# A list scheduler whose cost table counts more latency between engines and whose rule prefers matmuls of one shape

## The chip, the cores and the metric

One core of a Trainium2 chip runs the whole program. The metric is the device time of one execution in microseconds, as the median of several runs. The engines are PE (matmul), DVE, ACT, POOL, and SP, which here only issues DMA transfers.

## The reference

Attention with a mask by blocks of 64, and behind it a bilinear feed-forward network (FFN):

```python
# q, k, v: [8 batches, 8 heads, 576, 64], float32
scores = scale * np.matmul(q, k.transpose(0, 1, 3, 2))
mask = (pos[:, None] // 64) >= (pos[None, :] // 64)
scores = np.where(mask, scores, -1000000000.0)
attn = np.exp(scores - np.max(scores, axis=-1, keepdims=True))
attn = attn / (np.sum(attn, axis=-1, keepdims=True) + 1e-09)
x = np.matmul(attn, v)            # -> [4608 tokens, 512]
return ((x @ w_a) * (x @ w_b)) @ w_out      # d_ff = 1536
```

All sizes are float32; the kernel writes the output transposed, [512, 4608].

## The kernel before, in words

Products of the FFN are made in three matmuls each (hi by hi, hi by lo, lo by hi; `mm3`, with its matmul in L252), on operands split into a high and a low part. Attention's work is cut into 32 head pairs, four to a batch, numbered 0 to 31; a tile name such as `x2_6` says batch 2, head 6, which is pair 11. The first 10 pairs make their scores in plain float32 (matmuls `x2` in the rows of the order: two heads in one row), the later ones in three products (`x6`).

For one pair the steps are these. SP loads k and q (L420) and v (L425). ACT casts k (L485) and q (L477), POOL and DVE (L481) make the low parts; the first 10 pairs need no such cast. PE makes the scores in four blocks on 64 rows of its array: C3 (tile x, 512 keys) and C1 (tile y), then C2 (tile x, 448 keys) and C0 (tile y), all in L505. DVE takes maxima (L524, L540 and L541), ACT makes the exps e and e_s (L551), which also frees the score tile for a later block; DVE sums and inverts (L580 to L585), POOL scales e (L594). Pairs 0 to 4 then transpose e on PE (tile `tp`, L620) and ACT copies the result; from pair 5 on, DVE transposes 32 by 32 blocks (L599) and 16 transfers on SP's queue (L650, `at<-bl`, called D here) bring the blocks to their place. V, the product with v (L659, tile `av`, 60 half matmuls on 64 columns), ends the pair. ACT copies it out (L677, L678), ACT and POOL split it into xh and xl, and SP stores it (L692).

When a batch's four pairs are through, its FFN is made for 4 of 12 chunks of d_ff, in between the attention of later pairs: groups of four matmuls (`mm4`, in L714 to L729) that make tiles `ps0` and `ps1` (the products with w_a and w_b) and `pso` (with w_out). They have the lowest priority, so they fill PE where no step of attention is ready. The other 8 chunks make up a second stage, whose matmuls stand in L1065 and whose sums stand in L982 on DVE.

The order of all this is not written out but made by `plan()` (L360 to L406). Each operation is an `Op` with an engine, a list of those it depends on, a key (its priority) and a mode: 0 for the FFN and the transposes, 1 for scores (64 rows), 2 for V (64 columns). The table TOOK (L44 to L69) gives its duration and the lag until its result can be used. An operation is ready at the latest end of those it depends on, plus 0.3 us (SLACK) if it runs on PE and they don't. The planner goes forward in its own time, takes for the engine that comes first the ready operation of lowest key, and adds SWITCH where PE's mode changes. Every engine then runs its queue strictly in the planned order, at whatever pace the chip gives. `plan()` is called once for attention with the first part of the FFN (L938) and once, with `LOOK`, for the second stage (L1431), where all modes are 0. Between the two stands a piece of FFN whose order is written by hand.

Of the kernel before, what the change touches and what calls it, by code (L numbers as in the profile page):

```python
# [32 lines left out]
SLACK = 0.3  # L33
FIRST = 4
PET = 5
# [3 lines left out]
CONV_KEY = 12.0  # L39
CONV_LO = True  # L40
KEEP_UNTIL, KEEP_EVERY = 66.0, 2.5
SWITCH = 0.1
LAGS = {"PE": 0.24, "DVE": 0.14, "Activation": 0.17, "Pool": 0.1, "SP": 2.0}
TOOK = {  # L44
# [12 lines left out]
    "posta": (0.29, 0.17, 0), "postb": (0.375, 0.14, 0), "posto": (0.29, 0.17, 0), "hh": (0.338, 0.16, 0),  # L57
# [21 lines left out]
def attention_then_bilinear_ffn(  # L79
# [14 lines left out]
    DO, T = outT.shape  # L94
# [252 lines left out]
    PE_, DVE_, ACT_, POOL_, SP_ = LAGS  # L347
# [9 lines left out]
            self.n, self.frees, self.end = len(ops), None, None  # L357
            ops.append(self)

    def plan(look=0.0):  # L360
        free = dict.fromkeys(LAGS, 0.0)
        ready = {e: [] for e in LAGS}
        users = [[] for _ in ops]
        left = [len(o.deps) for o in ops]
        for o in ops:
            for d, plus in o.deps:
                users[d.n].append((o, plus))
            if not o.deps:
                ready[o.eng].append(o)
        out = []  # L370
        mode = 0
        bus = 0.0
        held = []

        def since(o):
            if not o.frees:
                return o.at
            if len(held) < MM:
                return o.at
            r = held[-MM]  # L380
            return o.at if r is o else 1e9 if r.end is None else max(o.at, r.end)

        while any(ready.values()):
            t, e = min((max(free[e], min(map(since, q))), e) for e, q in ready.items() if q)
            o = min((o for o in ready[e] if since(o) <= t + look), key=lambda o: (o.key, o.n))
            t = max(t, since(o))
            if o.frees:
                held.append(o.frees)
            ready[e].remove(o)
            free[e] = t + o.took + (SWITCH if e == PE_ and o.mode != mode else 0)  # L390
            if e == PE_:
                mode = o.mode
            if o.also:
                free[ACT_] = max(free[ACT_], t) + o.also
            o.start, o.end = t, free[e] + o.lag
            if o.kind in KB:
                bus = max(bus, t + LATENCY - 0.3) + KB[o.kind] / RATE
                o.end = bus + 0.3
            out.append(o)
            for u, plus in users[o.n]:  # L400
                u.at = max(u.at, o.end + plus + (SLACK if u.eng == PE_ and e != PE_ else 0))
                left[u.n] -= 1
                if not left[u.n]:
                    ready[u.eng].append(u)
        assert len(out) == len(ops)
        return out  # L406
# [37 lines left out]
    def got(what, p):  # L444
        return done.get((what, p))

    def attention(p):
# [9 lines left out]

        def add(what, eng, fn, deps=(), off=0.0, kind=None, **kw):
            deps = [(got(*d[:2]), *d[2:]) if isinstance(d, tuple) else (d,) for d in deps]
            done[what, p] = o = Op(kind or what, eng, fn, [(*d, 0.0)[:2] for d in deps if d[0]], key=B0 + off, **kw)  # L460
            return o

# [472 lines left out]
    for k in range(EARLY):  # L935
        o = Op("cv1", DVE_, lambda: next(box["g"]), [o, done["rc", NP - 1]], key=base[-1] + 20 + k)
    with tc.manual_schedule(engines={getattr(mybir.EngineType, e) for e in LAGS}):
        for o in plan():  # L938
            o.fn()
    conv2 = box["g"]  # L940
    lo_eng[0] = nc.vector
# [532 lines left out]
```

## Time and profile before

| what | us |
|---|---|
| median of 3 runs | 1134.1 (1132.92 to 1137.85) |
| profiled execution, its own time | 1138.72 |
| its span | 1136.9 |
| PE busy | 1096.3 (96%) |
| DVE busy | 871.4 (77%) |
| ACT busy | 630.0 (55%) |
| POOL busy | 402.7 (35%) |

The profiled execution is one that lies 4.6 us above the median of the runs; its mean granted PE clock is 0.987 of full speed. In the rows of a timeline stand start, duration, engine, line, operation, output and inputs with their sizes, the count, and in brackets the idle time ahead of it with what ended it. Line numbers are those of the kernel before.

### The profile page before, as it was taken

What the parts mean: (1) busy time and instruction counts of PE and PEld (TensorE: products, weight loads), DVE (VectorE), ACT (ScalarE), POOL (GpSimd) and SP (SyncE); (2) the same over time, 40 slices, a digit from 0 to 9 for tenths busy, and PEclk for the clock granted to TensorE, in tenths of its full rate; (3) what the DMA queues carried; (4) which work ended last, traced back from release to release, by engine and by line L of the source; (5) the groups of instructions that cost most, each with busy time, mean ns of one, the idle gap of its engine ahead of it and who ended that gap; (6) DMA issues with size and microseconds to landing.
All of it is one profiled execution on the core that took longest, in us unless ns stands there. A gap on an engine that the chain in (4) does not pass through costs nothing.

```text
span 1136.9 us, 23053 instructions
## 1 busy us (share of the span) xinstructions
PE 1096.3 (96%) x8356; PEld 1029.6 (91%) x8356; DVE 871.4 (77%) x1807; ACT 630.0 (55%) x1624; POOL 402.7 (35%) x593
## 2 busy tenths in 40 slices
PE   6889989999999999999999999999999999999997
PEld 3568778998988898899999999999999999999997
DVE  5888778776877777762899997787974877877856
ACT  4886566656665666662464654545543545545532
POOL 4687557664666556562100210202202022022020
PEclk7999989999999999999999999999999999999999
DMA  4553788877777887777433745737569245055052
GB/s 163 163 163 88 186 224 224 225 203 207 204 209 205 232 218 180 216 193 190 146 115 130 181 120 145 197 108 172 144 223 347 44 82 112 15 97 105 7 98 69
DMA packets 79024, 180.56 MB, mean 159 GB/s; under 512 B 13376, under 2 KB 34880, under 8 KB 78912
## 3 DMA queue, kind: packets, MB, share of 16 engines
q1 hardware_dynamic: 66240, 161.79, 48.5%
q0 software_dynamic: 12672, 17.31, 10.1%
q8 instruction: 66, 1.08, 0.4%
q14 instruction: 46, 0.38, 0.1%
HBM read 80.74 MB, written 48.76 MB: 114 GB/s over the span
## 4 chain that ended last, share of the span: by engine, by line
PE 58%; DVE 7%; DMA 6%; ACT 2%; SPq 2%; POOL 2%; issue 1%; ACTq 0%; POOLq 0%; DVEq 0%
PE bank L1065 46%; PE ps L252 5%; PE pso L252 3%; PE av L659 2%; DVE bl L599 2%; DMA kr<-kT 2%; DMA qr<-qT 2%; SPq L650 2%; DVE nm L524 1%; DMA at<-bl 1%; PE x L505 1%; POOL e L594 1%; PE y L505 1%; ACT e L551 1%; DVE xl L1017 1%
## 5 line engine op out<-in xcount | busy, mean ns | idle before, releaser
L1065 PE MATMUL bank<-xh,wab 128*128 128x384 f32 x1344 | 345.4, 334 | 0.8 <-DVE t L982 0.7
L1065 PEld LDWEIGHTS bank<-xh,wab 128*128 128x128 f32 x1344 | 243.0, 188 | 1.4 <-DVE t L982 1.0
L1171 POOL DMA_DIRECT2D outT<-pt x88 | 77.5, 1122 | 463.2 <-ACT pt L1329 275.7
L1065 PE MATMUL bank<-xl,wab 128*128 128x384 f32 x672 | 224.5, 334 | 0.0
L252 PE MATMUL ps<-xh,wab 128*128 128x288 f32 x1024 | 213.1, 298 | 0.0
L252 PEld LDWEIGHTS ps<-xh,wab 128*128 128x128 f32 x1024 | 165.4, 188 | 6.9 <-issue 5.5
L594 POOL TENSOR_SCALAR e<-e,rc 128x512 f32<-128x512 f32 (+3 forms) x256 | 150.5, 605 | 48.3 <-DVE rc L585 47.1
L252 PE MATMUL ps<-xl,wab 128*128 128x288 f32 x512 | 152.7, 298 | 0.0
L599 DVE STREAM_TRANSPOSE bl<-e 128x512 f32<-128x512 f32 (+1 forms) x216 | 116.4, 584 | 14.0 <-POOL e L594 12.7
L1065 PEld LDWEIGHTS bank<-xl,wab 128*128 128x128 f32 x672 | 126.1, 188 | 0.0
L982 DVE TENSOR_TENSOR u<-bank,u 128x384 f32<-128x384 f32 x158 | 87.8, 556 | 46.7 <-PE bank L1065 40.2
L1065 PE MATMUL bank<-hz,wo 128*128 128x384 f32 x612 | 109.9, 334 | 0.0
L1065 PEld LDWEIGHTS bank<-hz,wo 128*128 128x128 f32 x612 | 106.4, 188 | 0.0
L659 PEld LDWEIGHTS av<-at,v 128*64 128x64 f32 x1920 | 95.1, 140 | 8.4 <-issue 3.9
L659 PE MATMUL av<-at,v 128*64 128x128 f32 (+1 forms) x1920 | 100.2, 262 | 1.8 <-DMA at<-bl 1.1
L252 PE MATMUL pso<-hh,wo 128*128 128x288 f32 x480 | 101.3, 300 | 0.0
L252 PEld LDWEIGHTS ps<-xl,wab 128*128 128x128 f32 x512 | 96.1, 188 | 4.0 <-issue 3.4
L505 PE MATMUL x<-k,q 64*128 64x512 f32 (+1 forms) x344 | 65.7, 477 | 22.9 <-ACT e L551 18.7
L982 DVE TENSOR_TENSOR t<-bank,t 128x384 f32<-128x384 f32 x98 | 54.4, 555 | 38.8 <-ACT t L1108 20.3
L252 PEld LDWEIGHTS pso<-hh,wo 128*128 128x128 f32 x480 | 78.5, 190 | 3.2 <-issue 2.6
L524 DVE TENSOR_REDUCE nm<-x 128x2 f32<-128x1024 f32 x64 | 73.2, 1144 | 9.0 <-PE x L505 8.1
L551 ACT ACTIVATE e<-y,nm 128x192 f32<-128x192 f32 (+1 forms) x128 | 61.9, 486 | 22.0 <-DVE nm L524 18.5
(135 smaller groups left out, 1952.0 us busy)
## 6 DMA issues: line engine op xcount, KB each, us to landing
at<-bl SPq DMA_DIRECT2D x432, 112.0 KB, 2.3
xr<-xd SPq DMA_DIRECT2D x48, 384.0 KB, 4.2
outT<-pt POOLq DMA_DIRECT2D x88, 192.0 KB, 6.4
cv<-wab SPq DMA_DIRECT2D x24, 512.0 KB, 5.1
v<-vm SPq DMA_DIRECT2D x32, 320.0 KB, 3.2
xd<-xf SPq DMA_DIRECT2D x32, 288.0 KB, 2.5
outT<-ob SPq DMA_DIRECT2D x64, 144.0 KB, 2.1
wabd<-st SPq DMA_DIRECT2D x8, 896.0 KB, 5.8
```

The source lines that it names most:

```text
L252: nc.tensor.matmul(ps, w_, d_, start=(i == 0), stop=(i == n - 1))
L505: nc.tensor.matmul(out[:, h], qq[r, q0[t]:q0[t] + P], keys, start=j == 0, stop=j == len(qk) - 1)
L524: nc.vector.tensor_reduce(st["nm"][:, :, t], view, axis=AX.X, op=ALU.max, negate=True)
L551: nc.scalar.activation(out, view, AF.Exp, bias=bias, accum_out=sm[:, h, t, :1])
L594: nc.gpsimd.tensor_scalar(ev, ev, st["rc"][:, h, t:t + 1], 1.0, op0=ALU.mult, op1=ALU.mult)
L599: nc.vector.transpose(dst, es[h][t].rearrange("p (c g q) -> p c g q", g=NQ, q=QB))
L650: nc.sync.dma_start(st["at"][QB * g:QB * (g + 1), i], bl[QB * i:QB * (i + 1), g])
L659: nc.tensor.matmul(out[d], v[:, h, c], a[:, qs, h, e_], start=start, stop=stop, skip_group_check=True)
L982: return lambda: v.tensor_tensor(o, a, b, op=op)
L1017: lambda h_=h_, l_=l_, src=src, eng_=eng_: eng_.tensor_tensor(l_, src, f32(h_), op=ALU.subtract),
L1065: nc.tensor.matmul(banks[bk], a, b, start=start and not i, stop=i == 3 * n - 1, skip_group_check=not start)
L1171: do("acc", POOL_, lambda: nc.gpsimd.dma_start(part[o * P:(o + 1) * P, ts], t, accum_op=ALU.add), [name], [("part", o, 2 * tt_ + j)], key= ...
```

## The change

Three things change in the planner, and no operation is added or removed. First, the constants: SWITCH goes from 0.1 to 0.15 us, `mm4` from 0.528 to 0.532, and a new table CROSS adds 0.2 us to every edge from PE, DVE, ACT or POOL to another engine; edges from SP, the loads and copies, get 0.0. Second, `plan(stay=True)` for attention: while PE's mode isn't 0, it prefers an operation of the same mode that is ready within 0.3 us (STAY), then one of the other nonzero mode, and only then what the old rule takes. In mode 0 the new line, with HOLD at 0, takes what the old rule takes, apart from operations that aren't ready yet. Third, OFF can replace an operation's priority; it is empty and does nothing.

```diff
-SWITCH = 0.1
+SWITCH = 0.15
+STAY, HOLD = 0.3, 0.0
+CROSS = {"PE": 0.2, "DVE": 0.2, "Activation": 0.2, "Pool": 0.2, "SP": 0.0}
+OFF = {}
...
-"mm4": (0.528, 0.24, 0),
+"mm4": (0.532, 0.24, 0),
...
-    def plan(look=0.0):
+    def plan(look=0.0, stay=False):
...
             t, e = min((max(free[e], min(map(since, q))), e) for e, q in ready.items() if q)
-            o = min((o for o in ready[e] if since(o) <= t + look), key=lambda o: (o.key, o.n))
+            near = [o for o in ready[e] if since(o) <= t + look]
+            if e == PE_ and stay:
+                if mode:
+                    near = [o for o in ready[e] if o.mode == mode and since(o) <= t + STAY] or [
+                        o for o in ready[e] if o.mode and since(o) <= t + STAY] or near
+                else:
+                    near = [o for o in near if not o.mode or since(o) <= t - HOLD] or near
+            o = min(near, key=lambda o: (o.key, o.n))
...
-                u.at = max(u.at, o.end + plus + (SLACK if u.eng == PE_ and e != PE_ else 0))
+                u.at = max(u.at, o.end + plus + (SLACK if u.eng == PE_ and e != PE_ else 0) + (CROSS[e] if u.eng != e else 0))
...
+            off = OFF.get("Tb" if what == "T" and p < PET else what, off) if what not in ("V0",) else off
...
-        for o in plan():
+        for o in plan(stay=True):
```

In the rows below, the number ahead of the operation is its line; lines of the changed file are 3 to 11 higher than those of before. Numbers at the end of tile names only count tiles. What moves is shown at three places.

PE's queue at the scores of pair 6 (batch 1, head 4), before:

```order
L505 MATMUL x1_4_0_1136<-k1_4_880,q1_4_889 128x512 x2
L252 MATMUL ps1_0_0_1_1128<-xl0_2_0_616,wab1_83 128x288
L252 MATMUL ps1_0_0_1_1128<-xh0_2_0_615,wab1_83 128x288
L252 MATMUL ps1_0_0_1_1128<-xh0_4_0_797,wab1_83 128x288
L252 MATMUL ps1_0_0_1_1128<-xl0_4_0_798,wab1_83 128x288
L505 MATMUL y1_4_4_1156<-k1_4_880,q1_4_889 128x128 x2
L505 MATMUL y1_4_4_1156<-k1_4_880,q1_4_889 128x320 x2
```

and now:

```order
L516 MATMUL x1_4_0_1124<-k1_4_900,q1_4_905 128x512 x2
L516 MATMUL y1_4_1_1135<-k1_4_900,q1_4_905 128x128 x2
L516 MATMUL y1_4_1_1135<-k1_4_900,q1_4_905 128x320 x2
L255 MATMUL ps0_0_0_1_1116<-xl0_2_0_626,wab1_83 128x288
L255 MATMUL ps0_0_0_1_1116<-xh0_2_0_625,wab1_83 128x288
L255 MATMUL ps0_0_0_1_1116<-xh0_4_0_813,wab1_83 128x288
```

Four FFN products no longer stand between C3 and C1. At C1 the FFN is 16 products less far (four of ps0_0_0_1 are done where all twelve and eight of ps1_0_0_1 were), and at V(4) it is still 16 behind. Something of the same kind happens at pair 9 (batch 2, head 2): before, C3, V(6), C1, 12 products, C2, C0; now C3, C1, V(6), 20 products, C2, 4 products, C0.

PE's queue ahead of V(9), the product of pair 9 (av2_2), before:

```order
L252 MATMUL ps0_1_0_3_2359<-xh1_4_0_1808,wab3_85 128x288
L252 MATMUL ps0_1_0_3_2359<-xh1_6_0_1937,wab3_85 128x288
L252 MATMUL ps0_1_0_3_2359<-xl1_6_0_1938,wab3_85 128x288
L252 MATMUL ps0_1_0_3_2359<-xh1_6_0_1937,wab3_85 128x288
L659 MATMUL av02_2_2387<-at2_2_2135,v2_2_2042 64x64 x2
L659 MATMUL av2_2_2386<-at2_2_2135,v2_2_2042 64x128 x8
```

and now, with the last scores of pair 11 (batch 2, head 6):

```order
L255 MATMUL ps0_1_0_2_2302<-xl1_0_0_1310,wab2_84 128x288
L255 MATMUL ps0_1_0_2_2302<-xh1_0_0_1309,wab2_84 128x288
L255 MATMUL ps0_1_0_2_2302<-xh1_2_0_1544,wab2_84 128x288
L516 MATMUL y2_6_5_2309<-k2_6_2024,q2_6_2035 128x192 x6
L670 MATMUL av02_2_2321<-at2_2_2074,v2_2_2043 64x64 x2
L670 MATMUL av2_2_2320<-at2_2_2074,v2_2_2043 64x128 x8
```

Before, 32 FFN products stand between the last scores of pair 11 and V(9); now none does. 88 products stand between V(8) and V(9) before, 60 now. On SP's queue the loads of pair 12 stood ahead of the 16 copies of pair 9, and now stand behind them. On DVE the split of q for pair 13 (L481) stood ahead of pair 12's maximum (L524) and now stands behind all of pair 12's maxima.

ACT's queue at the exps of pair 16 (batch 4, head 0) and the cast of k for pair 17 (batch 4, head 2), before:

```order
L551 ACTIVATE e0_1_0_104,sm0_137<-y4_0_1_3438,nm4_0_3451 128x320
L756 CAST hh_2_0_3_3549<-hf_2_0_3_3534 128x288
L551 ACTIVATE e0_s_117,sm0_137<-y4_0_1_3438,nb4_0_3453 128x128
L485 CAST k4_2_3487<-kr4_2_3488 128x576
L551 ACTIVATE e0_1_1_108,sm0_137<-y4_0_1_3438,nm4_0_3451 128x320
```

and now:

```order
L562 ACTIVATE e0_1_0_104,sm0_137<-y4_0_4_3408,nm4_0_3397 128x320
L562 ACTIVATE e0_1_1_108,sm0_137<-y4_0_4_3408,nm4_0_3397 128x320
L496 CAST k4_2_3484<-kr4_2_3485 128x576
L488 ACTIVATE q4_2_3489<-qr4_2_3490 128x640
L562 ACTIVATE e0_2_0_105,sm0_137<-x4_0_5_3527,nm4_0_3397 128x448
```

Both exps of tile y now stand ahead of the cast. Casts of k that stand ahead of an exp of the first two blocks (e_3, e_1 or e_s) of the pair before are those of pairs 12, 17, 19, 24 and 28 before, and of pairs 14, 18, 19, 20, 24 and 28 now.

2 rows, old and new, of the table TOOK are left out of this document.

## The prediction

> **What bounds the kernel now.** I read the execution first by its stages, in a table of windows: start, end and length, then the busy time of PE, its weight load, DVE, ACT and POOL, then PE's granted clock. The stages are the opening, the front (pairs 5 to 9, up to the first FFN product of the second batch), the rest of attention, and the second stage.
>
> ```profile
> 0.00:80.00 80.00, 62.63 (x490) 40.91 (x492) 61.51 (x125) 57.90 (x175) 50.17 (x85) 0.91 0.49 159
> 80.00:158.30 78.30, 72.21 (x626) 58.41 (x624) 60.57 (x137) 48.41 (x156) 48.21 (x75) 0.93 0.59 161
> 158.30:533.70 375.40, 365.05 (x3705) 335.03 (x3703) 269.37 (x626) 223.27 (x709) 222.96 (x343) 1.00 0.78 208
> 533.70:1131.00 597.30, 596.30 (x3543) 595.26 (x3540) 478.33 (x918) 300.40 (x585) 81.38 (x92) 1.00 0.49 127
> ```
>
> PE is the bound everywhere but in the opening. Its idle time, most of what a new order can give back, is 78.30 − 72.21 = 6.1 us in the front, 375.40 − 365.05 = 10.4 us in the rest of attention and 597.30 − 596.30 = 1.0 us in the second stage. The front shows another loss: a clock of 0.93. So the next view was PE alone in narrow windows (length, PE's busy time, clock):
>
> ```profile
> 113.90:117.30 3.40, 1.54 (x11) 1.00 0.79 178
> 117.30:120.70 3.40, 3.40 (x17) 0.50 0.69 156
> 144.60:148.00 3.40, 1.14 (x9) 1.00 0.84 235
> 148.00:154.90 6.90, 5.54 (x42) 0.51 0.85 241
> 260.70:264.10 3.40, 1.35 (x20) 1.00 0.92 248
> 264.10:267.50 3.40, 3.40 (x41) 0.50 0.50 112
> ```
>
> Three times PE has under half of a 3.4-us window to do and runs the next window (once two) at half clock. A late operation thus costs its wait and then up to half of 3.4 us.
>
> **The change, part by part.** It adds and removes no instruction; the counts by engine are equal, and only the order differs. The larger SWITCH and the rule of the same shape ought to save changes of shape on PE. They hardly exist as a saving: counted in PE's order there are 203 stretches of one shape before and 202 after. From the timeline of PE (start, length) a change pair's price is seen where four FFN products stand between the two score blocks of pair 6:
>
> ```profile
> 93.01 1.13 PE L505 MATMUL x<-k,q 64*128 64x512 f32 x4
> 94.07 0.40 PE L252 MATMUL ps<-xl,wab 128*128 128x288 f32 x1
> ...
> 94.79 1.03 PE L505 MATMUL y<-k,q 64*128 64x128 f32 x8
> 99.41 0.42 PE L252 MATMUL ps<-xh,wab 128*128 128x288 f32 x2
> ...
> 99.81 0.43 PE L252 MATMUL ps<-xh,wab 128*128 128x288 f32 x2
> ```
>
> Three products in a row (two, and the one in the line left out) take 99.81 − 99.41 = 0.40 us, 0.133 each, so four take 0.53; between the score blocks they take 94.79 − 94.07 = 0.72. Two changes cost 0.19 us, one stretch fewer about 0.1: I put it at 0 (0 to −0.2). What counts is where the waits go.
>
> *The front.* The rows of PE, then of SP's queue (start, time over which the group was issued):
>
> ```profile
> 103.42 2.99 PE L659 MATMUL av<-at,v 128*64 128x64 f32 x60
> 116.31 1.02 PE L505 MATMUL x<-k,q 64*128 64x448 f32 x4 [1.86 <-ACT e L551]
> 123.11 2.98 PE L659 MATMUL av<-at,v 128*64 128x64 f32 x60
> 149.37 1.87 PE L505 MATMUL x<-k,q 64*128 64x448 f32 x4 [3.63 <-ACT e L551]
> 151.80 4.44 PE L659 MATMUL av<-at,v 128*64 128x64 f32 x60
> 156.17 0.97 PE L505 MATMUL x<-k,q 64*128 64x512 f32 x6
> 158.31 0.40 PE L252 MATMUL ps<-xh,wab 128*128 128x288 f32 x1
> ```
>
> ```profile
> 106.50 2.16 SPq L650 DMA_DIRECT2D at<-bl  x3
> 117.82 1.14 SPq L650 DMA_DIRECT2D at<-bl  x2
> 126.13 1.15 SPq L650 DMA_DIRECT2D at<-bl  x2
> 149.81 0.58 SPq L420 DMA_DIRECT2D kr<-kT  x1
> ```
>
> The sixteen copies D of pair 5 start when V of pair 4 ends (103.42 + 2.99 = 106.4) and are issued until 118.96 (117.82 + 1.14); those of pair 6 start when V of pair 5 ends (126.1), those of pair 7 follow without a gap until 149.8, and then come the loads that C3 of pair 10 needs at 156.17. This chain, V(4), D(5), V(5), D(6), D(7), loads and V(7), C3(10), sets the end of the front. What the new order moves in it:
> V(4) has 16 FFN products fewer ahead of it (the old order has come to the fourth matmul of ps1_0_0_3, the new to the last of ps1_0_0_2), 16 × 0.133 = 2.1 us, if C2(6) is ready for it. Between C1(6) and C2(6) stand 40 products before and after, and before C2(6) didn't wait. I take −1.8; if the exps that free the score tiles set the pace there, only the four products moved out from between C3 and C1 are left, −0.7.
> V(5) comes 123.11 − 118.96 = 4.2 us after the last issue of its copies, which land in 2.3 us in the median (below); so 1.9 us of it are not the DMA's, but come from the wait of 1.86 and the half clock behind it. In the new order 44 products stand ahead of C2(7) where there were 36: 8 × 0.133 = 1.06 of the 1.86 are filled, and the window is no longer under half. I take another −1.8, so V(5) and with it SP's 23.7 us of copies (126.1 to 149.8) move by −3.6.
> V(7) ran in the window of half clock, 4.44 us where V(5) took 2.98. In the new order the wait of 3.63 us in C2(9) is covered by 20 products and V(6), which now stand between C1(9) and C2(9) where 12 products stood. But PE that is early there only waits for D(7): what it gains is the slower clock's 1.5 us, and of these the loads of pair 10, which land no sooner than their queue lets them, leave perhaps 0.4. Front: −4.0 (−1 to −7; the far end takes V(7)'s 1.5 and the opening's operations too). The FFN work done by 158.31 is the same set in both orders, so this shift is a gain and not borrowed.
>
> ```profile
> at<-bl SPq DMA_DIRECT2D x432, 112.0 KB, 2.3
> ```
>
> *The middle.* The place with the largest loss, ACT's timeline and PE's:
>
> ```profile
> 261.44 0.67 ACT L485 CAST k<-kr 128x576 fp32r<-128x576 f32 x1 [2.30 <-DMA kr<-kT]
> 262.02 0.52 ACT L551 ACTIVATE e<-y,nm 128x320 f32<-128x320 f32 x1
> ```
>
> ```profile
> 262.69 0.58 PE L505 MATMUL y<-k,q 64*128 64x192 f32 x6 [2.05 <-ACT e L551]
> 263.20 4.92 PE L659 MATMUL av<-at,v 128*64 128x64 f32 x60
> ```
>
> A cast of k waits 2.30 us for its load at the head of ACT's queue; the exp behind it frees the tile for C0(16), which waits 2.05; then V runs at half clock, 4.92 − 2.98 = 1.9 lost. The new order puts both exps ahead of the cast: −3.9.
>
> At pairs 9 to 12 the order of three queues changes. Before, DVE takes its split of q of pair 13 ahead of pair 12's maximum, and the block C2(12) waits for the exps; now the split comes after it. Also, 32 FFN products stood between pair 11's last scores and V(9); now none does, and the loads of pair 12 come behind the sixteen copies of pair 9 instead of ahead of them. PE's rows and SP's:
>
> ```profile
> 184.56 2.98 PE L659 MATMUL av<-at,v 128*64 128x64 f32 x60
> 196.55 0.89 PE L505 MATMUL x<-k,q 64*128 64x448 f32 x6 [1.31 <-ACT e L551]
> ```
>
> ```profile
> 168.17 0.33 SPq L420 DMA_DIRECT2D kr<-kT  x1
> 169.23 1.78 SPq L650 DMA_DIRECT2D at<-bl  x3
> 177.47 4.90 SPq L650 DMA_DIRECT2D at<-bl  x7
> ```
>
> The 1.31 in C2(12) goes. But V(9) now has 60 products between V(8) and itself and not 88, so PE reaches it 28 × 0.133 = 3.7 us sooner, in the times of before at 180.8, while pair 9's copies end 169.23 − 168.17 = 1.1 us sooner, at 181.3, and land some 1.7 after the start of the last (2.3 from its issue): V(9) waits until about 183.0, 2.2 us. Twelve products and V(9) lie ahead of C3(12), 183.0 + 2.98 + 1.6 = 187.6; its loads, issued at 181.3, are ready for PE 156.17 − 149.81 = 6.4 later, at 187.7, so they add nothing. Net +0.9 (−1.3 if the copies are quicker, +2.6 with a half clock of 1.7 behind the wait).
>
> Then the casts. The planner counts nothing more for SP's loads (0.0), so it goes on putting casts of k at a time at which the load hasn't landed. Casts ahead of an exp of the pair before that belongs to its first two blocks, as at pair 17, are those of pairs 12, 17, 19, 24 and 28 before, and of 14, 18, 19, 20, 24 and 28 now: three new ones, 14, 18 and 20. The rows of the waits in this stage (total, times, longest):
>
> ```profile
> ACT k L485 <- DMA kr<-kT: 14.0, 11, 2.4
> PE x L505 <- ACT e L551: 3.0, 4, 1.3
> PE y L505 <- ACT e L551: 2.7, 2, 2.0
> ```
>
> Of the 22 casts of pairs 10 to 31, 11 wait; 14.0 / 22 = 0.64 is what one waits on average, and I let it reach PE in full, +1.9 for three; the ends are 0 and 3 × 2.4 = +7.2. Middle: −3.9 + 0.9 + 1.9 = −1.1. The near end takes pair 12's −1.3, no wait of the casts and the other waits of PE for an exp, 3.0 + 2.7 − 2.05 − 1.31 = 2.3: −7.5. The far end has +2.6 and casts of 1.1 each: +2.0.
>
> *The second stage.* PE's order there, 3540 matmuls, is word for word the same; CROSS only moves DVE's, ACT's and POOL's operations. PE's idle ahead of its costliest group shows the slack:
>
> ```profile
> L1065 PE MATMUL bank<-xh,wab 128*128 128x384 f32 x1344 | 345.4, 334 | 0.8 <-DVE t L982 0.7
> ```
>
> There is next to nothing to gain; an operation moved behind another can cost its 0.5 us a few times: +0.5 (−0.5 to +2). The opening is a chain between engines that the order hardly shortens: 0 (±0.3).
>
> Sum: −4.0 − 1.1 + 0.5 = −4.6. On the profiled execution's 1138.7 this gives 1134.1 (only by chance the number of the median); that execution lies 4.6 above the median of the runs, so against the median of 1134.1 the forecast is 1129.5. Its ends: −7 − 7.5 − 0.5 = −15, 1119, and −1 + 2 + 2 = +3, 1137.
>
> **The rivals.** First, half clock stays. Windows lie on a grid in time; shift PE's work by 2 to 4 us and other windows fall under half. Then the 1.9 us behind C0(16) and the 1.8 us of V(5) do not come back: −4.6 + 3.7 = −0.9, 1133.2. For it: the 10.4 us of idle in the middle stay spread, and SP's loads set the pace. Against it: the three windows above belong to single long waits that the new order covers. The Trainium skill ("TensorE: Matmul & The Clock Gate", Part 1, "HAM oscillation — how this bites in real kernels") gives as its abstract rule no PE idle gaps over about 3.4 us. By that rule waits of 1.86 and 2.05 us would not be what halves the clock, and shortening them would return the waits alone, which is this rival's sum; the rows above, with half clock after 1.54 and 1.35 us of work in 3.4, speak against the rule. Chance 0.17.
>
> Second, slower. The casts of k for pairs 14, 18 and 20 wait 2.4 us each at the head of ACT's queue, with C0 behind, and PE's window falls under half as it did at 262.69, 1.9 more each: 3 × 4.3 = 12.9 in place of 1.9, and the sum is −4.6 + 11.0 = +6.4, 1140.5. It decides where the load lands some 2 us or more after the cast's turn, at all three places. That 11 casts wait now speaks for it; that their mean is 1.27, and that only one place in the trace cost as much as 3.9, speaks against it. Chance 0.10.
>
> Third, all goes. If both half clocks, every wait of the exps and the casts' waits vanish, and the front reaches −6: −6 − 7.5 + 0.5 = −13, 1121. For it: in the new order V(6) and 20 products, 5.6 us, stand between C1(9) and C2(9), and 40 or more products between most others from pair 6 on, where pair 9 had 12, 1.6 us. Against it: the loads and V(9). Chance 0.22.
>
> That the rule of the same shape does little, as the count 202 has it, is not a rival but part of the sum: the time would come from CROSS.
>
> **How the numbers follow.** The forecast has 0.51, the rivals 0.17, 0.10 and 0.22. About 0.5% (5.7 us, 1128.4 and 1139.8) is what a measurement of this kernel can tell from no change. The forecast lies 1.1 above the first bound, so of its 0.51 somewhat under half, 0.23, is faster; with the third rival faster has 0.45, same 0.28 + 0.17 = 0.45, slower 0.10. The range 1119 to 1137 holds the forecast's ends, the first rival and the third, and leaves out the second.
>
> **What the profile will show.** Right: the first product of the second batch starts near 154 us instead of 158.31; V of pair 5 near 119.5; no clock of 0.50 from 117 to 155 and none after C0(16); the second stage as long as before within 2 us. Wrong: V(5) where it was, so that the front's chain starts earlier than I think; other windows at 0.50; no wait ahead of V(9); PE waiting over 2 us for an exp behind a cast of k at pairs 14, 18 or 20; idle of over 3 us on PE in the second stage.

## The result and the profile after

The changed kernel is slower. Its median over 10 runs is 1142.8 us (1137.9 to 1151.3) where the kernel before has 1136.4 (1132.9 to 1139.5) on the same chips; the ratio is 1.0067, with a 95% interval of 1.0046 to 1.0088 (that of the medians alone is 1.0056, inside it). The forecast was 4.6 us faster. The profiled execution took 1147.0 us (span 1145.2), 8.3 us of span more than the one of before. One execution of a kernel further down (`att_pe`) ran at a granted clock of 0.65 and took 1513.8 us, where its eleven others took 1134 to 1144; ratios and the table of starts leave it out.

Where the 8.3 us come from is read from the same table of windows as in the prediction, cut this time at events and not at times: the start of C3 of pair 6, the start of C3 of pair 10, the end of the last V, the end. Before (start and end, length, PE busy, weight load, DVE, ACT, POOL, PE's clock):

```profile
0.00:93.00 93.00, 75.23 (x576) 50.60 (x576) 73.13 (x147) 69.96 (x211) 60.58 (x99) 0.93 0.48 156
93.00:156.20 63.20, 57.72 (x523) 47.48 (x522) 47.97 (x111) 34.70 (x116) 37.19 (x59) 0.92 0.62 164
156.20:533.70 377.50, 366.95 (x3723) 336.27 (x3721) 270.35 (x630) 224.92 (x714) 223.57 (x343) 1.00 0.78 208
533.70:1136.90 603.20, 596.46 (x3543) 595.26 (x3540) 479.91 (x921) 300.40 (x585) 81.38 (x92) 1.00 0.49 128
```

And now, at the same events:

```profile
0.00:104.70 104.70, 81.96 (x566) 54.11 (x566) 73.75 (x149) 71.25 (x212) 63.17 (x99) 0.85 0.43 139
104.70:165.90 61.20, 56.85 (x533) 48.50 (x532) 46.34 (x113) 34.03 (x117) 37.83 (x61) 0.94 0.66 172
165.90:539.20 373.30, 364.65 (x3724) 334.64 (x3720) 268.79 (x626) 224.78 (x712) 221.23 (x342) 1.00 0.79 210
539.20:1145.20 606.00, 598.43 (x3544) 594.99 (x3540) 473.66 (x921) 300.28 (x585) 81.51 (x92) 1.00 0.48 127
```

The opening is 11.7 us longer, the front 2.0 shorter, the middle 4.2 shorter and the second stage with the hand-ordered piece before it 2.8 longer: 11.7 − 2.0 − 4.2 + 2.8 = 8.3. DVE, ACT and POOL are busy for as long as before in the opening, within 3 us; they have no more to do. On PE the 11.7 us are two things. Its idle time grows from 17.8 us (93.00 − 75.23) to 22.7 (104.70 − 81.96), by 5.0 us. Its busy time grows by 6.7 us, although 12 FFN products fewer (1.6 us) are done in it, and the granted clock falls from 0.93 to 0.85: PE does less work and does it more slowly.

The place where the largest part of it arises is the turn from pair 2 to pair 3. PE's timeline there (`...` stands for rows left out), before:

```profile
36.68 1.13 PE L505 MATMUL x<-k,q 64*128 64x512 f32 x4
37.64 0.93 PE L505 MATMUL y<-k,q 64*128 64x128 f32 x8
...
43.54 1.02 PE L505 MATMUL x<-k,q 64*128 64x448 f32 x4 [0.97 <-ACT e L551]
...
46.33 0.57 PE L620 MATMUL tp<-ident,e_s 128*128 128x128 f32 x2 [0.43 <-ACT at L626]
46.79 1.05 PE L914 MATMUL keep<-z 128*128 128x512 f32 x2
47.95 2.99 PE L659 MATMUL av<-at,v 128*64 128x64 f32 x60
50.86 1.13 PE L505 MATMUL x<-k,q 64*128 64x512 f32 x4
```

And after:

```profile
34.51 1.13 PE L516 MATMUL x<-k,q 64*128 64x512 f32 x4
35.57 2.99 PE L670 MATMUL av<-at,v 128*64 128x64 f32 x60
38.48 1.03 PE L516 MATMUL y<-k,q 64*128 64x128 f32 x8
...
44.93 1.02 PE L516 MATMUL x<-k,q 64*128 64x448 f32 x4 [1.53 <-ACT e L562]
...
49.36 0.45 PE L631 MATMUL tp<-ident,e_s 128*128 128x128 f32 x1 [0.46 <-ACT at L637]
49.54 2.93 PE L925 MATMUL keep<-z 128*128 128x512 f32 x4
52.40 4.94 PE L670 MATMUL av<-at,v 128*64 128x64 f32 x60
57.27 1.13 PE L516 MATMUL x<-k,q 64*128 64x512 f32 x4
```

C3 of pair 2 starts 2.2 us sooner than before and C3 of pair 3 6.4 us later: 22.8 us for the pair instead of 14.2. C3(2) has overtaken V(0), C1(2) comes behind V(0), C2(2) waits longer for an exp, the last transpose of pair 1 comes 3 us later, four keep matmuls instead of two stand ahead of V(1), and V(1) runs at half clock (4.94 us for 2.99). The waits come first here: C2(2) is already 1.4 us late when the clock halves at 46.3 us (windows below). On DVE one sees why the exps are late. Its timeline ahead of pair 2's exps, before:

```profile
37.86 1.23 DVE L524 TENSOR_REDUCE nm<-x 128x2 f32<-128x1024 f32 x1 [0.19 <-PE x L505]
...
39.82 1.16 DVE L524 TENSOR_REDUCE nm<-y 128x2 f32<-128x256 f32 x2
...
41.50 0.16 DVE L541 TENSOR_REDUCE nb<-nm 64x4 f32<-64x8 f32 x1
```

And after:

```profile
35.78 1.17 DVE L535 TENSOR_REDUCE nm<-x 128x2 f32<-128x1024 f32 x1
36.86 0.68 DVE L910 SCALAR_TENSOR_TENSOR cv<-cv 128x512 int32<-128x512 int32 x1
37.64 0.91 DVE L912 TENSOR_TENSOR cv<-cv 128x512 f32<-128x512 f32 x1
38.59 0.76 DVE L903 TENSOR_SCALAR cv<-cv 128x512 int32<-128x512 int32 x1
39.26 0.43 DVE L906 TENSOR_SCALAR cv<-cv 128x512 int32<-128x512 int32 x1
39.72 0.93 DVE L908 SCALAR_TENSOR_TENSOR cv<-cv 128x512 f32<-128x512 uint16 x1
...
41.39 1.16 DVE L535 TENSOR_REDUCE nm<-y 128x2 f32<-128x256 f32 x2
...
42.83 0.16 DVE L552 TENSOR_REDUCE nb<-nm 64x4 f32<-64x8 f32 x1
```

Between the maximum of tile x and that of tile y, where only three small clearings of y stood, DVE now makes five operations of a weight conversion (`cv`). Weights are converted in the opening, on DVE, ACT and POOL, with a lower priority than attention; the FFN's first product needs them. The maximum of y ends its row at 42.5 us where it ended at 41.0, though its x came 2 us sooner.

Windows of PE in the kernel after (start and end, length, PE busy, PE's clock):

```profile
42.80:46.20 3.40, 1.57 (x7) 1.00 0.50 161
46.30:56.50 10.20, 9.29 (x58) 0.50 0.39 129
77.00:80.40 3.40, 1.21 (x7) 1.00 0.02 7
80.40:83.80 3.40, 3.35 (x12) 0.50 0.00 0
155.50:158.90 3.40, 1.40 (x12) 1.00 0.86 238
158.90:165.70 6.80, 4.99 (x54) 0.50 0.94 252
```

Half clock now falls into the opening, where before it had none between 25 us and 117 us. In all, PE runs at half clock for 17.9 us between 25 us and C3(6) (the windows at 46 and 80 us and one at 97 us).

### The profile page after: what moved, and what is told of

Read it like the earlier page. It is cut to its first block, busy times and chain, and to the rows that moved or that the text cites. A ratio compares the mean times of both kernels' runs of the same rounds, so it can differ in the third digit from the quotient of the medians.

```text
span 1145.2 us, 23065 instructions
## 1 busy us (share of the span) xinstructions
PE 1101.9 (96%) x8356; PEld 1032.2 (90%) x8356; DVE 862.5 (75%) x1807; ACT 630.3 (55%) x1624; POOL 403.7 (35%) x593
## 4 chain that ended last, share of the span: by engine, by line
PE 48%; DVE 3%; DMA 0%; issue 0%; ACT 0%; POOL 0%; SPq 0%; DVEq 0%; POOLq 0%
PE bank L1076 45%; PE ps L255 2%; PE pso L255 1%; DVE xl L1028 1%; DMA pt<-outT 0%; DVE u L993 0%; DVE cv L216 0%; DVE hz L1129 0%; DVE t L993 0%; DVE cv L194 0%; DVE wab L223 0%; DVE cv L1152 0%; DVE cv L192 0%; DVE cv L1154 0%; DVE wo L1159 0%
## 5 line engine op out<-in xcount | busy, mean ns | idle before, releaser
L670 PEld LDWEIGHTS av<-at,v 128*64 128x64 f32 x1920 | 96.9, 142 | 14.2 <-issue 8.5
L670 PE MATMUL av<-at,v 128*64 128x128 f32 (+1 forms) x1920 | 102.5, 264 | 7.1 <-DMA at<-bl 6.0
L535 DVE TENSOR_REDUCE nm<-x 128x2 f32<-128x1024 f32 x64 | 73.5, 1148 | 12.0 <-PE x L516 10.8
L562 ACT ACTIVATE e<-y,nm 128x192 f32<-128x192 f32 (+1 forms) x128 | 62.2, 489 | 24.7 <-DVE nm L535 22.8
```

Of the source, the lines that this page charges most:

```text
L535: nc.vector.tensor_reduce(st["nm"][:, :, t], view, axis=AX.X, op=ALU.max, negate=True)
L562: nc.scalar.activation(out, view, AF.Exp, bias=bias, accum_out=sm[:, h, t, :1])
L670: nc.tensor.matmul(out[d], v[:, h, c], a[:, qs, h, e_], start=start, stop=stop, skip_group_check=True)
```

## The experiments

The theories that the runs were to tell apart were: A, the padded edges let low-priority work start ahead of attention's steps in the opening (A1, because a pair is stretched in the planner's clock, by which conversions are released; A2, because the plan leaves gaps, into which goes whatever is ready); B, the preference for the same shape made the bad order, by putting V(0) between two score blocks of pair 2; C, the phase of the clock's windows made the loss, whatever the order; D, half clock is what the loss consists of.

A time alone says little when the FFN has got further in one kernel than in another. So the table gives the start of C3 of pair 6 in each profiled execution, the number of FFN products done by then (40 before), and the delay against before for equal work: the difference of the starts plus 0.133 us for each product that is missing. The last column is the time at half clock between 25 us and C3(6), 0.2 us before. Each delay comes from one execution. The spread can be seen: the four profiles with the old rules in the opening (before, open_old, both_old, load_pad) start C3(6) at 91.9 to 93.5 us, the two of the whole change lie 2.6 us apart.

| kernel | ratio to before (95% interval) | C3(6), us | products | delay | half clock |
|---|---|---|---|---|---|
| whole change | 1.0067 (1.0046 to 1.0088) | 104.66 | 28 | 13.2 | 17.9 |
| whole change, second profile | one execution, 1148.2 us | 107.27 | 28 | 15.9 | 20.6 |
| cross_only | 1.0118 (1.0093 to 1.0143) | 102.41 | 40 | 9.4 | 13.7 |
| stay_only | 1.0075 (1.0050 to 1.0099) | 95.60 | 40 | 2.6 | 3.4 |
| open_old | 1.0003 (0.9986 to 1.0020) | 91.89 | 40 | −1.1 | 0.0 |
| open_new | 1.0104 (1.0084 to 1.0125) | 99.62 | 40 | 6.6 | 10.2 |
| conv_slow | 1.0059 (1.0037 to 1.0081) | 101.74 | 24 | 10.9 | 17.1 |
| look_open | 1.0098 (1.0066 to 1.0131) | 93.60 | 4 | 5.4 | 6.8 |
| keep_more | 1.0112 (1.0089 to 1.0135) | 99.83 | 0 | 12.1 | 13.7 |
| both_old | 0.9984 (0.9965 to 1.0003) | 93.09 | 40 | 0.1 | 3.4 |
| open_att | 1.0043 (1.0020 to 1.0066) | 102.13 | 24 | 11.2 | 7.9 |
| open_conv | 0.9987 (0.9971 to 1.0003) | 93.73 | 32 | 1.8 | 0.0 |
| keep_fill | 1.0448 (1.0420 to 1.0475) | 99.60 | 28 | 8.2 | 10.2 |
| load_pad | 0.9989 (0.9972 to 1.0006) | 93.46 | 40 | 0.5 | 0.9 |
| att_pe (start from att_pe2) | 1.0024 (1.0002 to 1.0046) | 94.63 | 28 | 3.2 | 3.4 |
| att_dve | 0.9984 (0.9959 to 1.0008) | 93.79 | 28 | 2.4 | 0.0 |
| att_act_pool | 1.0011 (0.9992 to 1.0030) | 96.59 | 28 | 5.2 | 4.2 |
| best | 0.9973 (0.9956 to 0.9991) | 93.47 | 36 | 1.0 | 0.0 |

**Which half of the change, and which part of the kernel.** CROSS alone, as in the kernel before otherwise (`mm4` too is back at 0.528):

```diff
-SWITCH = 0.15
+SWITCH = 0.1
-        for o in plan(stay=True):
+        for o in plan():
```

> Only the 0.2 us on edges between engines is kept; the cost of a shape change, the preference for the same shape and the cost of mm4 are as before. Theory A (the padding of the edges lets low-priority work, weight conversions above all, start ahead of attention's steps in the opening, and costs its 6 to 9 us there, by 105 us): still slower than before, 1.004 to 1.009 of it, with the scores of pair 6 starting at 100 us or later where they started at 93.0 before. Theory B (the preference for the same shape put V of pair 0 between the two score blocks of pair 2, and that delays the chain): 0.997 to 1.001 of before, pair 6 at 92 to 95 us. Theory C (half clock in the opening comes and goes by the phase of the clock's windows, whatever the order): no tie to the edit; windows of half clock before 105 us in some profiles of before too.

1.0118: the opening's loss is there without the rule of the same shape, and in this kernel's order too C3(2) has overtaken V(0). Theory A's place is right; the time is above its range. What is above lies behind the last V, where this kernel takes 6.5 us more than before for equal work. Part of that may be the counting, for by its last V it has made 92 FFN products more than the kernel before, and load_pad, with the old second stage and 96 more, comes out 3.3 us longer by the same count.

The other half alone, with SWITCH at 0.15 and `mm4` at 0.532:

```diff
-CROSS = {"PE": 0.2, "DVE": 0.2, "Activation": 0.2, "Pool": 0.2, "SP": 0.0}
+CROSS = {"PE": 0.0, "DVE": 0.0, "Activation": 0.0, "Pool": 0.0, "SP": 0.0}
```

> The extra 0.2 us is set to 0 everywhere; the preference for the same shape, SWITCH 0.15 and mm4 at 0.532 are kept. Theory A: as before or a little faster, 0.995 to 1.001, pair 6 at 92 to 95 us. Theory B: slower by what the whole change cost, 1.004 to 1.009, pair 6 at 100 us or later. Theory C: no tie to the edit.

1.0075, so theory A's time is missed, but so is B's place: the opening is 2.6 us late, not 10, and C3(2) stays behind V(0). The rest comes in the middle, where from C3(10) to the end of the last V, at equal work, this kernel takes some 11 us longer than before (in the profiled execution, the slowest of its six). Without the padded edges, the preference for the same shape, with the dearer change, makes the middle worse.

The old rules in the opening only (SWITCH is 0.1 there too), shown here, then the new ones in the opening only, with the conditions turned round:

```diff
-            if e == PE_ and stay:
+            if e == PE_ and stay and t >= 80:
...
-(CROSS[e] if u.eng != e else 0)
+(CROSS[e] if u.eng != e and (t >= 80 or not stay) else 0)
```

> The old rules until 80 us of the planner's own time, the new ones from there on and in the second stage. Theory A: the opening's loss is gone, the middle keeps 3 to 4 us of gain and the second stage its loss of 2: 0.996 to 1.000 of before, pair 6 at 92 to 95 us. Theory B says the same, since that place lies in the opening. Theory C: the opening differs from that of before by nothing but its luck, so pair 6 anywhere from 93 to 105 us and the time as that of the whole change, 1.004 to 1.009.

> The new rules until 80 us of the planner's own time, the old ones from there on and in the second stage. Theory A: the whole loss of the opening without the later gain: 1.006 to 1.010 of before, pair 6 at 100 us or later. Theory B: the same. Theory C: as before within 0.2%, whenever the phase is as before.

1.0003 and 1.0104. The opening's loss goes with the old rules and comes with the new ones, though in this one profile only to 6.6 us of the 13.2. Theory C falls, and the second profile of the whole change (below) says the same.

**What in the opening.** Conversions released more slowly, so that DVE's queue has as many of them ahead of each pair's maximum as before:

```diff
-CONV_STEP = 7.5
+CONV_STEP = 8.4
```

> The whole change, with weight conversions released every 8.4 us of the planner's time instead of 7.5, so that as many of DVE's conversion operations stand ahead of each pair's maximum as before the change (30 at pair 3, where the change has 35). Theory A1 (padding stretches a pair in the planner's clock, conversions are released by that clock, so they come ahead of the chain they should fill): pair 6's scores start at 94 to 99 us, 0.997 to 1.003 of before. Theory A2 (padding leaves gaps in the plan, and whatever is ready slips into them): pair 6 at 100 us or later, 1.004 to 1.009. Theory D (half clock in the opening makes the loss): tied to whether windows of half clock remain between 40 and 105 us.

C3(6) starts at 101.74 us, not at 94 to 99 as A1 had it: with 30 conversions ahead of pair 3's maximum, as before, most of the loss stays. That the delay falls from 13.2 to 10.9 us may be the spread, so whether the pace is a small part isn't shown. Look-ahead instead: an engine may wait 0.2 us for a more urgent operation rather than begin what is ready:

```diff
-            near = [o for o in ready[e] if since(o) <= t + look]
+            near = [o for o in ready[e] if since(o) <= t + (0.2 if stay and t < 80 else look)]
```

> The whole change, and until 80 us of the planner's time every engine may take an operation of higher priority that is ready within 0.2 us rather than start what is ready now. Theory A2: the opening's loss goes, pair 6 at 93 to 98 us, 0.997 to 1.002 of before. Theory A1: a stretched pair stays stretched, pair 6 at 100 us or later, 1.004 to 1.009.

Attention's chain is as early as before, C3(6) at 93.60, as A2 had it. But the time is 1.0098, which no theory had: now the conversions wait, 28 instead of 40 of DVE's stand ahead of pair 4's maximum, the first FFN product starts at 92.98 us instead of 83.45, and at C3(6) 4 products are done instead of 40. C3(2) and C1(2) stand ahead of V(0) here too, so overtaking V alone isn't the loss. At equal work the opening is still 5.4 us late: what attention gains, the FFN has lost. This profile, of 1143.1 us, is among the fastest of this kernel's executions (1143.0 to 1153.1), and its delay shrinks to 0.3 us by the last V; where the others lose more isn't shown. The opening thus has two chains, attention's and that of the conversions with the first FFN products, and a gain on one can cost the other.

Then the edges apart, in the kernel before, in attention's plan (`first`) until 80 us. CONVERSIONS stands for the nine kinds of operation that convert weights; the first line is open_att, the second open_conv:

```diff
+ (CROSS[e] if u.eng != e and first and t < 80 and u.kind not in CONVERSIONS else 0)
+ (CROSS[e] if u.eng != e and first and t < 80 and u.kind in CONVERSIONS else 0)
```

> The kernel before, with the 0.2 us added until 80 us of the planner's time only on edges that lead to an operation of attention, not on those that lead to a weight conversion. Theory A2 (the plan holds attention's next step back by 0.2 us per edge, and whatever is ready, conversions on DVE, ACT and POOL and keep matmuls on PE, is put into the gap, where on the chip there is less room than planned): the whole loss of the opening, pair 6's scores at 99 us or later, 1.004 to 1.010 of before. If the loss comes from stretching the chain of the conversions: pair 6 at 92 to 95 us, 0.998 to 1.002.

> The kernel before, with the 0.2 us added until 80 us of the planner's time only on edges that lead to a weight conversion. Theory A2: nothing is held back but the low-priority work, pair 6 at 91 to 95 us, 0.998 to 1.002 of before. If the loss comes from stretching the chain of the conversions, and with it the first product of the FFN: pair 6 at 99 us or later or the first product 3 us or more later than 83.5, 1.003 to 1.010.

C3 of pair 6 with the edges to attention padded, from PE's timeline:

```profile
102.13 1.13 PE L516 MATMUL x<-k,q 64*128 64x512 f32 x4 [0.59 <-ACT e L562]
```

And with the edges to the conversions padded:

```profile
93.73 1.13 PE L516 MATMUL x<-k,q 64*128 64x512 f32 x4
```

This is the cleanest pair: 11.2 us of delay against 1.8, 1.0043 against 0.9987. A2 holds; stretching the conversions' own chain costs nothing that can be told from the spread. With the edges to attention padded, C3(2) has again overtaken V(0), and 45 conversions instead of 40 stand ahead of pair 4's maximum on DVE; with the others it is 40, as before.

By the engine on which the padded edge ends, here PE; the other two kernels name DVE, and ACT and POOL, in its place:

```diff
+ (CROSS[e] if u.eng != e and first and t < 80 and u.eng == PE_ and u.kind not in CONVERSIONS else 0)
```

> The kernel before, with the 0.2 us added until 80 us of the planner's time only on edges from another engine to a step of attention on PE. Planned, the order of PE's blocks in the opening stays that of before. If the gaps on PE (keep matmuls, blocks that overtake V) make the loss: pair 6's scores at 98 us or later, 1.003 to 1.008 of before. If the queues of DVE, ACT and POOL make it: 92 to 95 us, 0.998 to 1.002.

> The same with only the edges to a step of attention on DVE (the maxima, sums). Two more conversion operations stand ahead of each maximum than before, where the whole change has five. If the conversions on DVE make the loss: pair 6 at 96 to 100 us, in proportion or more, 1.001 to 1.006. If those on ACT and POOL make it: 92 to 95 us, 0.998 to 1.002.

> The same with only the edges to a step of attention on ACT or POOL (the exps and the copies of transposes, the scaling). Here C3 of pair 2 overtakes V of pair 0 on PE, as with the whole change. If the queues of ACT and POOL make the loss: pair 6 at 98 us or later, 1.003 to 1.008. If it is PE's or DVE's edges: 92 to 95 us, 0.998 to 1.002. If all three engines' edges add up: each of the three runs between, 94 to 97 us.

> A second profile of the kernel with only the edges to attention's steps on PE padded, whose first profiled execution ran with PE's clock at 0.65 from end to end. By its times (1.0024 of before) and if PE's edges are a part of the loss: pair 6's scores at 95 to 99 us. If its loss lies elsewhere: 92 to 95 us.

The delays are 3.2 (PE, from the second profile), 2.4 (DVE) and 5.2 us (ACT and POOL), together 10.8 of the 11.2 with all. That they add up so well is luck in part: each is one execution, and the second profile of `att_pe` took 1132.5 us, less than any of the eleven executions behind its ratio. What is shown is that no one engine's edges bring the whole loss; ACT's and POOL's bring the most in these profiles, and of the three it is there that C3(2) overtakes V(0). The times don't follow the delays: 1.0024 for PE, 0.9984 for DVE, 1.0011 for ACT and POOL, and they don't add up to 1.0043.

**Half clock.** More keep matmuls, first ahead of the FFN in priority, then (the second piece as well, and 0.43 for 0.24 in the table) behind it and planned at their measured length:

```diff
-KEEP_UNTIL, KEEP_EVERY = 66.0, 2.5
+KEEP_UNTIL, KEEP_EVERY = 100.0, 1.25
...
-        o = Op("keep", PE_, keep_on, at=4 + k * KEEP_EVERY, key=1e5)
+        o = Op("keep", PE_, keep_on, at=4 + k * KEEP_EVERY, key=2e6)
```

> The whole change, with the matmuls that keep the clock up issued twice as often and until 100 us of the planner's time instead of 66. Theory D: no half clock between 30 and 105 us, pair 6 at 93 to 97 us, 0.998 to 1.003 of before. Theories A1 and A2: the half clock goes and pair 6 still starts at 99 us or later, 1.002 to 1.008, since PE isn't what the opening waits for.

> The whole change, with the matmuls that keep the clock up planned at their measured 0.43 us, released twice as often and until 100 us of the planner's time, and behind the FFN's products in priority. Theory D (half clock makes the opening's loss): fewer windows of half clock before 105 us, and C3 of pair 10, 9.7 us late with the change, is at most 4 us late; 1.000 to 1.004 of before. Theory A2: C3 of pair 10 still 6 us late or more, 1.003 to 1.009.

Neither decides. In the first, the half clock from 46 to 56 us is there as with the whole change, and C3(3) starts at 57.32 us where it starts at 57.27 there. From 56 us to 250 us PE keeps full clock, and C3(3) to C3(6) take 42.5 us, where the change takes 47.4 and the kernel before 42.2. But the keep matmuls push out the FFN, whose first product starts at 115 us, so this stretch holds no FFN product, where it holds 28 with the change and 40 before. In the second, V of pair 8 starts only at 220.5 us: since V of pair 7, 288 FFN products and 36 keep matmuls stand ahead of it. With the FFN spent so early, PE idles for 27.6 us between C3(10) and the last V, where the change has 8.7, and half clock comes back until 283 us; so the 1.0448 comes from what follows the opening.

What can be read directly is how the loss is made up. At the turn above, V(1) takes 4.94 us for 2.99, and four keep matmuls 0.73 each for 0.53, 2.8 us together of the 8.6 that the pair lost there. Over the whole opening, the 13.2 us at equal work are some 5.0 us of waits and some 8.3 of PE at work for longer (6.7 and the 1.6 of the missing products). The half clock accounts for these, by an estimate: PE is busy for 9.29 and 3.35 us in the two stretches of half clock above and for 3.41 in the one at 97 us, and at full clock this work would take half as long, 8.0 us less. With the edges to attention alone (open_att) the same sum gives 6.8 us of waits and 4.4 of slower work. So theory D is right about the larger part of the loss with the whole change. But half clock isn't a cause apart from the order: with at most 3.4 us of it in the last column every delay is at most 3.2 us, with 4.2 us or more every delay is at least 5.2, and all kernels with the old rules in the opening are in the first group, all with the whole padding there in the second. The two columns don't grow in step, though, and what would be left of the loss at full clock isn't shown, since PE might then only wait longer.

A second profile of the whole change:

> A second profile of the whole change. If the opening's loss is in the order: pair 6's scores again at 100 us or later, also with other windows of half clock. If the windows make it: its start moves with how many of them fall before 105 us, and with two fewer it lies at 98 us or earlier.

C3(3) and C3(6) in it:

```profile
59.84 1.13 PE L516 MATMUL x<-k,q 64*128 64x512 f32 x4
...
107.27 1.13 PE L516 MATMUL x<-k,q 64*128 64x512 f32 x4
```

The order loses again at the same pair, from 35.41 to 59.84 us, with half clock at other times.

**The rest of the kernel.** The second stage by the old rules too:

```diff
-(CROSS[e] if u.eng != e and (t >= 80 or not stay) else 0)
+(CROSS[e] if u.eng != e and t >= 80 and stay else 0)
```

> The old rules until 80 us of the planner's time and in the second stage, the new ones in the rest of attention only. If the extra 0.2 us is what lengthens the second stage: that stage has the length of before, 3 us less than in the run with only the opening's rules old, and the time is 0.995 to 0.999 of before. If the second stage's length comes from elsewhere (what attention leaves it): still 3 us longer than before, 0.998 to 1.002.

From the end of the last V this kernel takes 603.5 us, the one with only the opening's rules old 606.5, before 603.2. So CROSS costs the second stage 3.0 us. The loads (1.0 us more on edges that leave SP), for which my prediction had blamed the planner:

```diff
-"Pool": 0.2, "SP": 0.0}
+"Pool": 0.2, "SP": 1.0}
```

> As the run with the new rules in the middle alone, with 1.0 us more counted on the edges that leave SP, from 80 us of the planner's time on. If casts that wait for their loads at the head of ACT's queue cost PE time in the middle, as the prediction had it: ACT's waits of k for its load fall from 18 us in the middle to under 8, the middle shortens by 2 to 4 us, 0.994 to 0.998 of before. If PE's work covers those waits: the waits fall and the time stays, 0.997 to 1.001.

ACT's waits for k's load go from 18.0 to 16.3 us and the time stays. One extra microsecond doesn't take these waits away, and so it remains open what they cost.

The harmless parts together: the new rules in the middle, the padding of the conversions' edges in the opening, the old second stage.

```diff
-(CROSS[e] if u.eng != e and t >= 80 and stay else 0)
+(CROSS[e] if u.eng != e and stay and (t >= 80 or u.kind in CONVERSIONS) else 0)
```

> The new rules in the middle only, as in the run that was the fastest, and in the opening the 0.2 us only on edges to a weight conversion; the second stage by the old rules. The two parts measured 0.9984 and 0.9987 of before one by one. If they add up: 0.995 to 0.999. If the earlier opening is lost again in the front, where SP's copies set the pace: 0.997 to 1.000.

0.9973 (0.9956 to 0.9991): by the ratio some 3 us faster than the kernel before, and by more than that faster than the kernel after. Its interval overlaps those of both_old and open_conv, so that the parts add up isn't shown.

## Why the prediction was wrong, point by point

**The step that failed** is one sentence of the prediction, a term put at nothing: "The opening is a chain between engines that the order hardly shortens: 0 (±0.3)". I had asked only whether a new order can shorten a chain, and not whether it can lengthen it. The order of the queues, which I had read for the front, differs in the opening too: 35 of DVE's conversion operations stand ahead of pair 3's maximum instead of 30, and C3(2) ahead of V(0). Neither sign makes the loss alone (conv_slow has 30, look_open has C3(2) ahead), but they were reason enough not to put the term at nothing. In its place stand 11.7 us, 13.2 at equal work: 5.0 us of waits and 8.3 us of PE working more slowly, both started by the padded edges to attention's steps (open_att 11.2 us, open_conv 1.8). That is larger than the whole forecast, and none of my rivals named it; the slower one, with its chance of 0.10, was about casts of k, which isn't what happened.

**The front.** I forecast −4.0; from C3(6) to C3(10) it is 61.2 us instead of 63.2, and in it 12 FFN products more are done (212 instead of 200, 1.6 us), so −3.6 for equal work. That it comes so close is luck in part. The wait of 1.86 us in C2(7) and the half clock that stood behind it at 117 us are gone, and from C3(6) to V(5) it takes 25.4 us instead of 30.1 (−4.7 for a forecast of −3.6); but from V(5) to C3(10) it takes 35.9 instead of 33.1, where the forecast had −0.4. As foretold, PE now waits for the copies of pair 7 instead:

```profile
156.56 0.34 PE L670 MATMUL av<-at,v 128*64 128x64 f32 x4
160.71 5.28 PE L670 MATMUL av<-at,v 128*64 128x128 f32 x56 [3.81 <-DMA at<-bl]
```

I had not seen how long this wait would be, nor that half clock comes again with it (158.9 to 165.7 in the windows above): V(7) takes 5.28 us behind the wait, where it took 4.44.

**The middle.** I forecast −1.1 with ends −7.5 and +2.0; it is −4.2. C0(16) has no wait and no half clock follows it; PE's idle time falls by 1.9 us, its busy time by 2.3. V(9) waits, as worked out, 1.69 us for 2.2:

```profile
188.85 0.34 PE L670 MATMUL av<-at,v 128*64 128x64 f32 x4
190.87 2.87 PE L670 MATMUL av<-at,v 128*64 128x128 f32 x56 [1.69 <-DMA at<-bl]
```

The term that was mis-sized is that of the casts. They do wait more, 20.2 us in 17 places instead of 14.0 in 11, but PE's own waits for exps stay small and about as they were. The rows of after for this stage:

```profile
ACT k L496 <- DMA kr<-kT: 20.2, 17, 2.7
PE y L516 <- ACT e L562: 3.3, 5, 1.2
PE x L516 <- ACT e L562: 3.1, 5, 1.0
```

So there is no sign that the +1.9, which I had let reach PE in full, reached it.

**The second stage.** I forecast +0.5 with an end of +2; it is +2.8, shown to be CROSS by both_old. PE's order being the same said nothing about the order of the others, and I took the small idle time of before as a sign that little could change, where it only says that little can be gained.

**The shape changes.** 203 and 202 stretches: next to nothing was to be had there; stay_only shows that the rule, with the dearer change, can even do harm by the order that it makes.

**Half clock elsewhere.** My first rival, that windows of half clock move and don't vanish, came true in its condition and not in its price: they went from 117, 148 and 264 us to 46, 80, 97 and 159 us, but the rival's time was 1133.2 us, for it too had the opening unchanged. The Trainium skill ("TensorE: Matmul & The Clock Gate", Part 1, "HAM oscillation — how this bites in real kernels") warns of PE idle gaps over about 3.4 us; here the clock halved at 46.3 us behind a window with 1.57 us of work in 3.4 and no wait longer than 1.53 us, so the measurement disagrees with that bound, as before.

## What to carry to other kernels

A greedy list scheduler answers a larger latency not by waiting but by starting what is ready: padding the edges of a chain puts low-priority work into gaps that are not there on the chip, and where the chain is the limit, as in this kernel's opening, that lengthens it, and here half clock came with the longer waits. In the middle, where PE is the limit, padding and preference together gained 2 to 4 us in the profiles (open_old 2.1, both_old 3.7, the change 4.2, at equal work) and the padding alone 0.9 (cross_only); the time of both_old, 0.9984 (0.9965 to 1.0003), can't quite be told from no change. So such costs belong to a stage, or to the edges of the work that may wait (here the conversions), and the length of the latency-bound stage is to be forecast first, in both directions.

## What the runs showed of the hardware that I had not expected

Runs of one order spread by more than the effect: 1137.9 to 1151.3 us for the change. Its two profiles, of the same order, had half clock at 46, 80, 97 and 159 us, and at 35, 49, 83, 100 and 162 us.
